# Two rules of buffer and order in the backward pass of a decode block: which free slot a tile takes, and how far dV runs ahead of dK

## The chip, the cores and the metric

The kernel runs on one core of a Trainium2 chip. The metric is the device time of one execution in microseconds (us), the median of several executions; the profile is one more execution, seen by the hardware profiler. The engines are named as in the profile: PE is TensorE, DVE is VectorE, ACT is ScalarE, POOL is GpSimd, and SP is SyncE, which here only issues transfers (its queue is written SPq).

## The reference

The reference runs one decode step of a pre-norm transformer block and takes its gradients. Four sequences (`B = 4`) have one new token each, and each of 32 heads has a cache of 4096 keys and values of width 128:

```python
q = (layernorm(x) @ wq)                       # one query a head and sequence
p = softmax(q . k_cache * Dh**-0.5)           # 4096 weights a head
h = x + (p @ v_cache) @ wo
out = h + (silu(ln(h) @ w1) * (ln(h) @ w3)) @ w2
_out, _vjp = jax.vjp(_f, A_x, A_k_cache, A_v_cache, A_wq, A_wo, B_w1, B_w3, B_w2)
```

It returns `out` and the gradients of all eight inputs. Two of these are as large as the caches: dV (`out_3`) and dK (`out_2`), 4 x 32 x 4096 x 128 in bf16, 1.05 MB (1024 KB) for each of the 128 pairs of sequence and head, which the kernel calls heads. For one head both are outer products: dV is the column p times the row dO (the gradient of the attention output), and dK is the column dS times the row q. dS needs V: dP = V dO, and dS = p (dP - c) scale with a number c for each head. So dV of a head can be made without loading anything, while dK of a head needs V of that head first.

## The kernel before

The forward half (until about 660 us) streams K and V once. A short middle part does the feed-forward block and its backward. The second half, from about 690 us on, loads V once more and writes dV and dK. All large transfers are issued by SP, in the order of the program, on one queue.

**Slots.** All large tiles lie in one SBUF array, `arena`, cut into 23 slots of 8320 bytes a partition (`NSLOT`, `SLOT`). A slot holds one head of K, V, dV or dK. `free` is a list of free slots in the order in which they were given back. `Slot` takes one slot, `Slot2` two neighbouring ones. `give` puts slots at the end of the list as soon as their last use has been written into the program, not when it is over; whoever takes the slot next gets a wait for the work that still holds it. For a slot that held dV or dK this is the landing of the write to HBM.

`Slot` takes the head of the list. While `part["B"]` is set it first calls `lone_slot`, which moves another slot to the head of the list: it prefers the ends of runs of free slots that have an odd length, so that neighbouring slots stay together as pairs for `Slot2`. `Slot2` takes, of the free pairs that its rule allows, the one whose later slot has been free for longest.

**The steps.** Heads 0 to 23 (`SP = 24`) are handled one by one, heads 24 to 127 in 52 pairs (`NT`), which halve the number of transfers and of DVE instructions. `load_V2` loads V of one head, `load_pair` that of two. `front` (or `front_pair`) transposes V on PE, 8 blocks at a time, copies each group of 8 back with ACT (L803 and L804, L1274 and L1275), and multiplies by dO for dP (L1208, L1289). `group_dS` and `group_dS_pair` make dS of four heads on DVE from a transpose of dP that a later `front` puts on PE (`rows_T`). `grad_V` and `grad_K` take a slot, make the outer product with one DVE instruction (`outer`, L809) and issue the write (L820, L1232). `grad_pair` does this for two heads (`outer_pair`, L1355; the write is L1365).

The order of the second half is written out by hand. First five fronts run, with dV of heads 2 to 8 between them. Then step `s` (heads 0 to 23) does: load V, `front(s + 5)`, `more_V(...)`, `grad_K(s)`, and dS at each fourth head. From step 19 on, every second step does the front of a pair. Then step `t` (the 52 pairs) does: loads, `front_pair(t + 3)`, `more_V(...)`, `grad_pair` for dK, and dS at each second pair. `more_V(upto)` writes dV until it is `upto` heads far, and its argument is the number of dK heads done so far plus `lead_V(s)`. `side` adds the small remaining work (the gradient of the weights and of x) between the steps; its outputs go through two-slot tiles (`staged`, L1071).

**What sets the order.** Nothing is rearranged after this: each engine runs its instructions in program order. DVE therefore stops at an outer product whose slot is still being written out, and all later DVE work stops with it. SP stops at a load whose slot is still in use, or at a write whose outer product is not done.

Of the kernel before, what the change touches and what calls it, by code (L numbers as in the profile page):

```python
# [21 lines left out]
SP = 24  # L22
# [3 lines left out]
def kernel(  # L26
# [25 lines left out]
    B = A_x.shape[0]  # L52
# [55 lines left out]
    part = {"B": False}  # L108
# [723 lines left out]
    def load_V2(eng=nc.sync):  # L832
        s = nv["next"]
        if s < SP:
            V2s[s] = Slot("V2", vring if vring else free)
            eng.dma_start(out=V2s[s].heads(), in_=cache_head(A_v_cache, s))
            nv["next"] += 1
# [128 lines left out]
    with ExitStack() as c2:  # L966
# [185 lines left out]
        def replicate(nm_, i0):  # L1152
            if i0 >= NH or (nm_, i0 // REP) in reps:
                return
            K_ = 8 * B if i0 < 8 * B else P
            rows = dOrows_bf if nm_ == "rdo" else qrows_bf
            ps = psrep.tile([P, REP, Dh], FP32, tag="rep", name="rep_ps")
            for i in range(REP):
                nc.tensor.matmul(ps[:, i, :], lhsT=ident_b[0:K_, i0 + i:i0 + i + 1].to_broadcast([K_, P]), rhs=rows[0:K_, :],
                                 start=True, stop=True)  # L1160
            rt = rep_bufs[nm_][i0 // REP % 2]
            nc.scalar.copy(out=rt, in_=ps[:])
            reps[nm_, i0 // REP] = rt
# [28 lines left out]
        def front(s):  # L1192
            hl = s % B
            if s not in VTs:
                for g in range(SJ // GW):
                    V_T(s, psT, range(g, g + 1))
                    if hl == 0 and g == 0:
                        rows_out()
                    if hl == 0 and g == 2:
                        rows_T()  # L1200
            VT = VTs[s].heads()
            if hl == 0:
                rows["acc"] = psD.tile([P, 512], FP32, tag="dP", name="dP_ps")
            dO_window(s + 2)
            for u in range(2):
                for c in range(4):
                    j0 = 8 * c + 4 * u
                    nc.tensor.matmul(rows["acc"][32 * c:32 * (c + 1), :], lhsT=zq_window(zd[hl], 2 * hl + u),  # L1208
                                     rhs=VT[:, j0:j0 + 4, :], start=(hl == 0 and u == 0),
                                     stop=(hl == B - 1 and u == 1), tile_position=(0, 32 * c))  # L1210
            if hl == B - 1:
                rows["ps"] = rows.pop("acc")
            sl = VTs.pop(s)
            (vring if nv["next"] < SP and len(V2s) + len(VTs) + len(vring) < NV2 else free).append(sl.i)

        def group_dS(g):
            i0 = g * B
            T = rows.pop("T").rearrange("p jj (c m) -> p c m jj", c=4)
            t = rows.pop("t")[:, 0:B * SJ].rearrange("p (b j) -> p b j", b=B)
            t5 = t.rearrange("p b (c u jj) -> p b c u jj", c=4, u=2)  # L1220
            for hl in range(B):
                nc.vector.tensor_scalar(out=t5[:, hl], in0=T[:, :, 2 * hl:2 * hl + 2, :], scalar1=c_rep[:, i0 + hl:i0 + hl + 1],
                                        scalar2=scale, op0=ALU.subtract, op1=ALU.mult)
            dS2s[g] = bw3.tile([P, B, SJ, 2], BF16, tag="dS2", name="dS2", bufs=1)
            nc.vector.tensor_tensor(out=dS2s[g][:], in0=t[:, :, :, None].to_broadcast([P, B, SJ, 2]),
                                    in1=P_all[:, i0:i0 + B, :, None].to_broadcast([P, B, SJ, 2]), op=ALU.mult)

        def grad_K(s):
            b, h = bh_of(s)
            gk = Slot("gk")  # L1230
            outer(gk.heads(), dS2s[s // B][:, s % B], reps["rq", s // REP][:, s % REP, :])
            nc.sync.dma_start(out=rows_of(out_2[b, h]), in_=gk.heads())  # L1232
            gk.give()

        def prefetch():
            while nv["next"] < SP and vring:
                load_V2(nc.sync)
# [21 lines left out]
        def load_pairs(t):  # L1259
            while npv["next"] < NT and (npv["next"] <= t or len(pV) < 3 and len(Slot2.choices()) > 1):  # L1260
                load_pair()

        def dO_pair(t):
            if t < NT:
                s, s2 = two(t)
                nc.gpsimd.tensor_copy(out=zt[t % B][:, 32:34], in_=dOT_bf[:, s:s2 + 1:B])

        def front_pair(t, mid):
            pl = t % 2
            v = pV[t].t[:, 0:2 * SJ * Dh].rearrange("p (j d) -> p j d", d=Dh)  # L1270
            for g in range(2 * SJ // GW):
                pt = psT.tile([P, GW, P], BF16, tag="tps", name="pt_tps")
                for i in range(GW):
                    nc.tensor.transpose(pt[:, i, :], v[:, g * GW + i, :], ident_b[:])  # L1274
                nc.scalar.copy(out=v[:, g * GW:(g + 1) * GW, :], in_=pt[:])  # L1275
                if pl == 0 and g == 0:
                    rows_out()
                if pl == 0 and g == 2:
                    rows_T()
                if g == 3:  # L1280
                    mid()
            if pl == 0:
                rows["acc"] = psD.tile([P, 512], FP32, tag="dP", name="dP_ps")
            dO_pair(t + 2)
            for u in range(4):
                m = 8 * pl + 2 * u
                for c in range(4):
                    j0 = 16 * c + 4 * u
                    nc.tensor.matmul(rows["acc"][32 * c:32 * (c + 1), :], lhsT=zt[t % B][:, 32 - m:64 - m], rhs=v[:, j0:j0 + 4, :],  # L1289
                                     start=(pl == 0 and u == 0), stop=(pl == 1 and u == 3), tile_position=(0, 32 * c))  # L1290
            if pl == 1:
                rows["ps"] = rows.pop("acc")
            pV.pop(t).give()
# [38 lines left out]
        def replicate_pair(nm_, q):  # L1332
            if q >= NT // B or (nm_, "p", q) in reps:
                return
            s = SP + q * 2 * B
            K_ = 8 * B if s + 2 * B <= 8 * B else P
            rws = dOrows_bf if nm_ == "rdo" else qrows_bf
            ps = psrep.tile([P, REP, Dh], FP32, tag="rep", name="rep_ps")
            for i in range(REP):
                for a in range(2):  # L1340
                    n = s + i + a * B
                    nc.tensor.matmul(ps[64 * a:64 * (a + 1), i, :], lhsT=ident_b[0:K_, n:n + 1].to_broadcast([K_, P // 2]),
                                     rhs=rws[0:K_, :], start=True, stop=True, tile_position=(0, 64 * a))
            rt = rep_bufs[nm_][(H0 + q) % 2]
            nc.scalar.copy(out=rt, in_=ps[:])
            reps[nm_, "p", q] = rt
# [45 lines left out]
                    replicate_pair("rdo", t // B + 1)  # L1392

        def lead_V(s):
            return 8 - min(4, max(0, s - 56) // 4)

        def load_ahead(s):
            prefetch()
            if s < SP and s not in V2s and s not in VTs:
                load_V2(nc.sync)  # L1400

        def side(s):
            if O0 <= s < S0:
                step("o")
            if s >= S1:
                step("s", 2)
            elif s >= O0:
                step("q")

        part["B"] = True  # L1410
        for s in range(2):
            dO_window(s)
        for s in range(3, 6):
# [9 lines left out]
                replicate("rdo", REP)  # L1423
        group_dS(0)
        for s in range(SP):
            load_ahead(s + L)
            if nv["next"] >= SP:
                load_pairs((s + L - SP) // 2)
            if s % REP == 2:
                if s + 2 < SP:  # L1430
                    replicate("rq", s + 2)
                else:
                    replicate_pair("rq", 0)
            if s + L < SP:
                front(s + L)
            elif (s + L - SP) % 2 == 0:
                if s + L == SP:
                    dO_pair(0)
                    dO_pair(1)
                front_pair((s + L - SP) // 2, lambda: None)  # L1440
            if s > 0:
                more_V(s + 1 + lead_V(s))
            grad_K(s)
            if s % B == B - 1:
                if s + 1 < SP:
                    group_dS((s + 1) // B)
                else:
                    group_dS_pair(0)
            side(s)
        for t in range(NT):  # L1450
            s = SP + 2 * t
# [46 lines left out]
```

## Time and profile before

Three executions gave a median of 1730.34 us (1726.66 to 1730.5); the profiled one has a span of 1731.4 us.

| what | number |
|---|---|
| HBM read and written | 422.59 MB and 282.34 MB, 407 GB/s over the span |
| busy share of the 16 DMA engines, SP's queue | 98.1% |
| PE busy | 1240.6 us (72%) |
| DVE busy | 1231.9 us (71%) |
| ACT busy | 959.4 us (55%) |
| DVE outer product, one head (L809) | 2.29 us |
| DVE outer product, one pair (L1355) | 4.42 us |
| share of the chain that ended last: DMA out_dram<-arena | 38% |

The busy share of DMA is a mean of 16 engines; the GB/s beside it tell whether the engines moved data at the pace that they show elsewhere. A stretch in which the pace is lower is one in which time is lost for good, if the transfers are what the kernel must wait for. The chain that ended last is followed back from the last instruction; a step "DMA out_dram<-arena" in it means that an instruction waited for a write to HBM to land.

### The profile page before, as it was taken

The page shows a single profiled execution, that of the slowest core. Times are in us where ns is not written, and L with a number is a line of the kernel's source. Part 1 is how long each engine was busy: PE and PEld are TensorE (multiplying, and loading weights), DVE is VectorE, ACT ScalarE, POOL GpSimd, SP SyncE. Part 2 cuts the span into 40 slices and gives each one's busy share as a digit, 9 for nine tenths or more (in the row PEclk, how much of TensorE's full clock was granted, in tenths as well). Part 3 has the DMA queues.
Part 4 walks back from the last instruction along what each step waited for, and adds up shares of the span by engine and source line. Part 5 has one row for each costly group of instructions (what it writes and reads, how often), then busy time and mean ns, then how long its engine had stood idle before and what let it go on. Part 6 is the DMA issues. An engine that isn't in the chain of part 4 may idle for free.

```text
span 1731.4 us, 37799 instructions
## 1 busy us (share of the span) xinstructions
PE 1240.6 (72%) x16232; PEld 954.3 (55%) x16232; DVE 1231.9 (71%) x1190; ACT 959.4 (55%) x1489; POOL 318.3 (18%) x575
## 2 busy tenths in 40 slices
PE   5889888888888889766788655666656756766550
PEld 4677766677667667544566544544434434444340
DVE  5999899989999995456586666565546475475584
ACT  3555455445455445565667466666657656655540
POOL 2211222322222221102103021012003011011030
PEclk9999999999999998897878689867788666666865
DMA  9999999999999999699989999999999999999997
GB/s 401 424 425 424 424 423 425 423 423 424 417 420 407 424 413 401 251 385 385 427 362 425 430 427 428 428 426 430 426 396 406 427 419 401 414 407 401 402 406 337
DMA packets 78264, 707.45 MB, mean 409 GB/s; under 512 B 8444, under 2 KB 12680, under 8 KB 14224
## 3 DMA queue, kind: packets, MB, share of 16 engines
q1 hardware_dynamic: 77680, 704.94, 98.1%
q8 instruction: 127, 2.08, 0.5%
q14 instruction: 41, 0.34, 0.0%
q0 software_dynamic: 416, 0.10, 0.0%
HBM read 422.59 MB, written 282.34 MB: 407 GB/s over the span
## 4 chain that ended last, share of the span: by engine, by line
DMA 41%; DVE 13%; issue 3%; PE 3%; ACT 1%; DVEq 0%; SPq 0%; POOL 0%; ACTq 0%
DMA out_dram<-arena 38%; DVE arena L1355 8%; DMA arena<-in_A_v_cache_dram 4%; DVE arena L809 3%; ACT arena L1275 1%; PE M_ps L475 1%; DVE arena L460 1%; PE pt_w L604 1%; PE pt_tps L1274 0%; ACT Pn L439 0%; DVEq L1493 0%; PE kP_ps L485 0%; DVE dPr L1302 0%; PE gu_ps L876 0%; PE dn_ps L907 0%
## 5 line engine op out<-in xcount | busy, mean ns | idle before, releaser
L1275 ACT COPY arena<-pt_tps 128x1024 bf16<-128x1024 bf16 x416 | 400.2, 1023 | 234.1 <-PE pt_tps L1274 233.5
L1274 PE MATMUL pt_tps<-ident_b,arena 128*128 128x128 bf16 x3328 | 328.2, 269 | 223.8 <-DMA arena<-in_A_v_cache_dram 147.7
L1274 PEld LDWEIGHTS <-arena 128*128 128x128 bf16 x3328 | 282.1, 124 | 321.4 <-DMA arena<-in_A_v_cache_dram 168.9
L1355 DVE TENSOR_TENSOR arena<-arena 128x8192 bf16<-128x8192 bf16 x52 | 230.0, 4423 | 183.9 <-DMA out_dram<-arena 168.3
L1355 DVE TENSOR_TENSOR arena<-dS,arena 128x8192 bf16<-128x8192 bf16 x52 | 230.0, 4425 | 120.9 <-DMA out_dram<-arena 120.7
L475 PE MATMUL M_ps<-arena 128*128 128x130 bf16 x4096 | 286.4, 222 | 35.4 <-DMA arena<-in_A_v_cache_dram 35.2
L460 DVE TENSOR_TENSOR arena<-arena 128x4096 bf16<-128x4096 bf16 x128 | 292.5, 2285 | 24.7 <-POOL arena L456 23.6
L475 PEld LDWEIGHTS <-arena 128*128 128x128 bf16 x4096 | 253.4, 99 | 55.7 <-DMA arena<-in_A_v_cache_dram 48.6
L367 DVE STREAM_TRANSPOSE arena<-arena 128x512 f32<-128x512 f32 (+1 forms) x321 | 250.7, 797 | 0.0
L362 ACT COPY arena<-pt_tps 128x1024 bf16<-128x1024 bf16 x128 | 129.4, 1012 | 183.5 <-PE pt_tps L361 145.1
L1352 POOL COPY arena<-arena 128x128 bf16<-128x128 bf16 x52 | 78.1, 1502 | 562.3 <-ACT arena L1329 300.9
L373 POOL TENSOR_TENSOR W<-qrep,wmask 128x128 bf16<-128x128 bf16 x128 | 121.0, 945 | 85.3 <-PE S_ps L393 70.7
L456 POOL COPY arena<-P_all 128x64 bf16<-128x64 bf16 x128 | 32.7, 255 | 412.5 <-ACT P_all L450 409.5
L804 ACT COPY arena<-pt_tps 128x1024 bf16<-128x1024 bf16 x96 | 91.9, 1024 | 19.5 <-PE pt_tps L803 19.3
L1289 PE MATMUL dP_ps<-arena 128*32 128x512 bf16 x832 | 91.4, 473 | 9.2 <-ACT arena L1275 9.1
L803 PE MATMUL pt_tps<-ident_b,arena 128*128 128x128 bf16 x768 | 64.9, 244 | 32.9 <-ACT arena L804 27.9
L450 ACT COPY P_all<-pt_P 32x64 bf16<-32x64 bf16 x256 | 52.1, 203 | 54.1 <-PE pt_P L446 51.9
L361 PE MATMUL pt_tps<-ident_b,arena 128*128 128x128 bf16 x1024 | 80.5, 223 | 0.0
L485 PE MATMUL kP_ps<-arena,onesw 128*32 128x512 bf16 x1024 | 79.2, 386 | 0.0
L803 PEld LDWEIGHTS <-arena 128*128 128x128 bf16 x768 | 56.0, 112 | 41.3 <-issue 40.0
L809 DVE TENSOR_TENSOR arena<-P,arena 128x4096 bf16<-128x4096 bf16 x21 | 48.0, 2290 | 43.2 <-DMA out_dram<-arena 43.0
L809 DVE TENSOR_TENSOR arena<-dS,arena 128x4096 bf16<-128x4096 bf16 x24 | 54.9, 2295 | 31.6 <-DMA out_dram<-arena 31.5
(245 smaller groups left out, 1534.5 us busy)
## 6 DMA issues: line engine op xcount, KB each, us to landing
out_dram<-arena SPq DMA_DIRECT2D x108, 2048.0 KB, 21.5
arena<-in_A_v_cache_dram SPq DMA_DIRECT2D x152, 1024.0 KB, 15.5
arena<-in_A_k_cache_dram SPq DMA_DIRECT2D x128, 1024.0 KB, 15.4
arena<-in_A_v_cache_dram SPq DMA_DIRECT2D x52, 2048.0 KB, 24.4
out_dram<-arena SPq DMA_DIRECT2D x48, 1024.0 KB, 8.1
arena<-in_A_wq_dram SPq DMA_DIRECT2D x8, 1024.0 KB, 17.3
arena<-in_B_w_dram SPq DMA_DIRECT2D x8, 896.0 KB, 15.5
out_dram<-arena SPq DMA_DIRECT2D x3, 1792.0 KB, 25.2
```

The costliest lines, as they stand in the source:

```text
L362: nc.scalar.copy(out=KT[:, c * GW:(c + 1) * GW, :], in_=pt[:])
L367: nc.vector.transpose(out=KT[:, c * w_:(c + n) * w_], in_=Kn[:, c * w_:(c + n) * w_])
L373: nc.gpsimd.tensor_tensor(out=W[:, hl], in0=qrep[:, :, s:s + 1].to_broadcast([P, 4, 32]), in1=wmask[:, hl, None, :].to_broadcast([P, 4, 32 ...
L460: nc.vector.tensor_tensor(out=PK[:, :, 0:Dh].rearrange("p j (r t) -> p j r t", t=2), in0=Ks[s].heads().rearrange("p j (r t) -> p j r t", t=2),
L475: nc.tensor.matmul(hold["M"][:], lhsT=Vn[:, j, :], rhs=PK[:, j, :], start=(j == 0), stop=(j == SJ - 1))
L803: nc.tensor.transpose(pt[:, i, :], v[:, g * GW + i, :], ident_b[:])
L804: nc.scalar.copy(out=v[:, g * GW:(g + 1) * GW, :], in_=pt[:])
L809: nc.vector.tensor_tensor(out=dst.rearrange("p j (r t) -> p j r t", t=2), in0=col2[:, :, None, :].to_broadcast([P, SJ, Dh // 2, 2]), in1=r ...
L1274: nc.tensor.transpose(pt[:, i, :], v[:, g * GW + i, :], ident_b[:])
L1275: nc.scalar.copy(out=v[:, g * GW:(g + 1) * GW, :], in_=pt[:])
L1289: nc.tensor.matmul(rows["acc"][32 * c:32 * (c + 1), :], lhsT=zt[t % B][:, 32 - m:64 - m], rhs=v[:, j0:j0 + 4, :], start=(pl == 0 and u == ...
L1355: nc.vector.tensor_tensor(out=dst.rearrange("p (j r t) -> p j r t", r=Dh // 2, t=2), in0=col2[:, :, None, :].to_broadcast([P, 2 * SJ, Dh / ...
```

## The change

The change has two parts.

1. `part["B"]` was set to true ahead of the first step of the second half and stayed so. Now it is set in each step `s` of the single heads, to `s + 12 >= SP`. So in the five fronts before the steps, and in the steps 0 to 11, `Slot` takes the slot that was given back first; from step 12 on (twelve heads ahead of the change to pairs) and through all pairs, `lone_slot` chooses as before. It is for a longer time between the write of a slot and the next use of that slot.
2. `lead_V(s)` was 8 heads up to head 56 and went down to 4 from head 72 on. Now it is 8 to the end. dV of the later heads is made two pairs earlier, and the last steps have dK alone.

```diff
         def lead_V(s):
-            return 8 - min(4, max(0, s - 56) // 4)
+            return 8
...
-        part["B"] = True
         for s in range(2):
             dO_window(s)
...
         group_dS(0)
         for s in range(SP):
+            part["B"] = s + 12 >= SP
             load_ahead(s + L)
```

No transfer, no outer product and no matmul is added or removed. What differs is which slot a tile lies in, what its first instruction has to wait for, and in what order dV, dK and loads follow each other from head 60 on.

## The prediction

> **What bounds the kernel now.** I first read the DMA row of the page, then cut the span into stretches, then looked at the chain of waits where a stretch is slow. The stretches (length; busy us and count of PE, PE weight load, DVE, ACT and POOL; granted clock; DMA share; GB/s):
>
> ```profile
> 700.00:740.00 40.00, 27.18 (x268) 17.49 (x266) 19.70 (x17) 26.28 (x30) 7.47 (x24) 0.83 0.62 236
> 740.00:840.00 100.00, 67.56 (x751) 49.71 (x746) 63.69 (x47) 58.89 (x67) 18.56 (x25) 0.85 0.99 394
> 840.00:920.00 80.00, 61.39 (x654) 47.90 (x655) 50.31 (x37) 51.31 (x60) 6.92 (x18) 0.81 0.95 394
> 920.00:1240.00 320.00, 208.84 (x2188) 156.52 (x2186) 197.13 (x105) 201.55 (x238) 62.53 (x47) 0.79 1.01 428
> 1240.00:1320.00 80.00, 49.00 (x544) 33.16 (x542) 49.50 (x28) 53.62 (x67) 13.35 (x13) 0.84 0.97 398
> 1400.00:1660.00 260.00, 164.10 (x1421) 113.49 (x1419) 147.03 (x67) 156.11 (x199) 22.67 (x29) 0.69 1.00 407
> ```
>
> For 320 us the transfers run at 428 GB/s with every engine under 70%: the second half is bound by transfers. I use 428 GB/s as the pace that can be had. Time lost in a stretch is its length times (1 - GB/s / 428): 18 us in 700 to 740, 8 in 740 to 840, 6 in 840 to 920, 6 in 1240 to 1320, 13 in 1400 to 1660. The first is by far the densest, and the chain of waits there (start, length, what) is
>
> ```profile
> 702.63 7.46 DMA out_dram<-arena
> 710.22 2.30 DVE arena L809
> 712.53 3.85 DMA out_dram<-arena
> 716.51 2.30 DVE arena L809
> 718.83 3.85 DMA out_dram<-arena
> 722.80 2.30 DVE arena L809
> 725.12 3.93 DMA out_dram<-arena
> 729.17 2.30 DVE arena L809
> ```
>
> An outer product, its write to HBM, then the next outer product: strictly in turn. DVE waits for the write that still holds its slot. I followed the free list through both programs (bookkeeping, in which no time enters) and numbered SP's transfers from 0; dV of head 0 is number 279. Before, numbers 281, 282 and 283 (dV of heads 2, 3, 4) all take slot 0, each right behind the last. Up to number 310 dV and dK then alternate mostly between slots 0 and 2, used again 2 to 4 transfers later, mostly 3. The waits in 700 to 740 say the same (engine, line, for what: us, times, longest):
>
> ```profile
> DVE arena L809 <- DMA out_dram<-arena: 19.8, 6, 7.5
> ACT arena L1162 <- DVE arena L809: 3.7, 1, 3.7
> ```
>
> The first line is the wait for slots; the second is a knock-on, a row replica that ACT can't overwrite before the late DVE has read it, and PE's transposes wait behind it.
>
> **What the Trainium skill says.** (1) "Perfetto Trace Analysis", section "Optimization Strategy": the same gap again and again on the engine that should be full can mean that there was no buffer for the next tile. The trace agrees: three waits of 3.85 to 3.93 us in a row. (2) "DMA: Bandwidth & Descriptors", section "Anatomy of one DMA": about 2.0 us fixed, mostly the receipt of the last byte, beside bytes over 436 GB/s; waits are taken by the issuing sequencer, never by the DMA engines. Here a lone write of 1.05 MB lands after 3.85 us, which at 428 GB/s is 2.45 us of data and 1.40 us fixed; I use the trace. (3) The same page, section "Queues, rings and completion order": descriptors are consumed in ring order. So the depth of SP's queue counts: a wait for a landing is hidden while other transfers stand in the queue. The 3.85 us waits stand where it was empty; later pair loads took 24.4 us (median) to land, a full queue.
>
> **Part 1, first slots in order of being freed: 700 to 740.** Now numbers 281 to 285 rotate over slots 10, 11 and 0, used again 3 transfers later. One turn of a slot is 2.30 us of DVE and 3.85 us to the landing; three slots give one head each (2.30 + 3.85) / 3 = 2.05 us, under the 2.45 us that its data takes. So the transfers become the bound here too. Until 709 the queue is full in any case with loads of V. From there numbers 281 to 290, seven dV and three V, need 10 x 2.45 = 24.5 us, to 733. The next, dK of head 0 (number 291), needs dS of the first group, thus the transposes in front 4. Undisturbed fronts start 5.0 us apart (730.35 and 735.35 before); front 1 starts at 704.96 as before, so front 4 at 720 to 721, its `rows_T` at 724, dS 0.72 + 0.42 us later, dK issued at 728, 5 us ahead of the drain. Before it was issued at 745.18. I count 3 of the 18 us as still lost: **-15 us**.
>
> **Part 1, 740 to 840.** Numbers 287 to 324 are now used again after 6 to 9 transfers (before: 3 for most, 4 to 6 from 311 on). Each step moves one dV, one dK and one V: 3 x 2.45 = 7.35 us. DVE needs 2 x 2.30 us and a quarter of 1.14, 4.9 us. PE and ACT need 6.3 us for a front with its side work (fronts started at 754.10, 760.40 and 767.09 when nothing held them up), so they keep ahead by about 1 us a step, with three bundles of dO columns of some 3 us each to take out of it over 19 heads. Neither is the bound, though with little room. The stretch 920 to 1240, where slots come back after 6 or 7 transfers, loses nothing. I take 5 of the 8 us: **-5 us**.
>
> **Part 1, 840 to 920.** From number 333 to 412 both programs have the same transfers in the same slots, with uses again after 3 to 5 transfers at the change to pairs. This stretch should come some 20 us earlier and lose its 6 us again: 0.
>
> **Part 2, the lead.** Two dV pairs move from the end to the steps of heads 60 and 68. Before, the second of these steps has one write only (issued at 1270.29), and the next dV takes the slots of a weight gradient written 3 transfers earlier:
>
> ```profile
> 1289.37 4.42 DVE L1355 TENSOR_TENSOR arena<-arena 128x8192 bf16<-128x8192 bf16 x1 [19.11 <-DMA out_dram<-arena]
> 1274.08 0.90 ACT L1096 COPY arena<-pt_Tr 4x896 bf16<-4x896 bf16 x1 [14.64 <-DMA out_dram<-arena]
> ```
>
> DVE waits 19.11 us and the queue runs dry from 1290 to 1296 (153 to 286 GB/s, some 3 us lost). Now the step has two writes, and it is a load (number 428) that takes these slots. That adds a wait to SP: the load waits for the landing of number 425, and the writes 429 and 430 stand behind it, with DVE's later slots. When 425 lands, 426 and 427 (2 x 4.9 us of data) are still queued, so the DMA engines should not run dry. ACT's wait of 14.64 us stays: in both programs the slot of `rows1` was given back 2 transfers earlier, and fronts queue behind it. I take **-2 us**, between -3 (the whole gap) and +5 (SP's wait shows).
>
> Elsewhere in the pairs slots come back after 4 or 5 transfers in both programs, so I leave the 13 us of 1400 to 1660 as they are. **The tail**: before, ten writes follow the last load, now eight. The last load was issued at 1660.14, its transposes began at 1681.28 and its `rows_T` ended at 1692.1, 32 us after the issue. Now six outer products and one dS stand between load and last dS, 28.8 us after the issue; DVE waits 3 us, and the last dK is issued 42.5 us after the load. The queue, which before drained at 1722, 62 us after the load, drains two writes sooner, at 52 us. So 9 us of room stay; 0.
>
> **Sum**: 1730.3 - 15 - 5 - 2 = 1708 us.
>
> **The rivals.** *A, given back later.* The early gain only makes the transfers arrive at a slower place: PE and ACT with 1 us a step of room, or the short reuse at 333 to 342, where the queue drains deeper. Then half of the 15 us and nothing of the 5 stay: 1730.3 - 8 = 1722. For it: 20 us are gained on engines whose room is small; against it: 320 us at 428 GB/s behind it. *B, the late pace too.* 1400 to 1660 has a DMA share of 1.00 and yet 407 GB/s, with the lead at 4; 920 to 1240 had 428 with the lead at 8. If the lead is the cause, most of the 13 us come on top: 1708 - 11 = 1697. Against it: 1320 to 1400 ran at 427 GB/s with the lead at 4 already. *C, not faster.* The first half of A, and SP's load wait or the thin tail costs as much as the rest brings: 1730. *D, slower.* PE's fronts set the pace from 740 on, so that nothing early remains, and SP's wait and an unhidden tail cost 5 us each: 1740.
>
> **How the numbers follow.** Forecast 0.60, A 0.14, B 0.12, C 0.06, D 0.08. The predicted time is the forecast's, 1708. The range takes in A and B with some room for the +5 of part 2 and for a run's spread: 1694 to 1725. Faster is forecast, A and B: 0.86; within 0.3%: 0.06; slower: 0.08.
>
> **What would show it.** In 700 to 740 the pace should be near 400 GB/s, the slot waits of L809 down from 19.8 us to some 8, and the first dK (L1232) issued near 728. 740 to 820 should run above 410 GB/s. The load that waits on SP should show beside a DMA share of 1.0. If PE is the bound in 740 to 840, PE's idle time vanishes there and the pace stays below 400: then A. The prediction is wrong if 700 to 740 is fast and the span is not some 15 us shorter, or if the end of the chain becomes dS.

## The result, and the profile after

| kernel | median us (lowest to highest) | ratio to before [95% interval] |
|---|---|---|
| before | 1730.42 (1726.66 to 1730.88) | |
| changed | 1704.17 (1697.57 to 1709.01, 4 runs) | 0.985 [0.981, 0.990] |
| changed, measured again | 1707.07 (1699.05 to 1709.31, 4 runs) | 0.986 [0.984, 0.988] |

The forecast was 1708 us. One thing to keep in mind below: the eight times of the changed kernel lie in two groups, three from 1697.6 to 1699.6 and five from 1706.2 to 1709.3, and both profiles taken of it (spans 1707.2 and 1707.5 us) belong to the second.

The stretches of the changed kernel, with the columns of the table in the prediction (length; busy us and count of PE, PE weight load, DVE, ACT, POOL; granted clock; DMA share; GB/s):

```profile
700.00:740.00 40.00, 29.23 (x310) 19.15 (x308) 29.25 (x22) 29.36 (x34) 16.05 (x27) 0.88 0.97 389
740.00:840.00 100.00, 78.21 (x863) 58.64 (x861) 61.29 (x47) 68.86 (x80) 23.94 (x31) 0.90 1.01 426
840.00:920.00 80.00, 62.83 (x718) 48.64 (x718) 60.90 (x38) 55.61 (x65) 17.36 (x13) 0.87 0.96 395
920.00:1240.00 320.00, 208.85 (x2092) 155.30 (x2091) 192.61 (x103) 197.44 (x236) 39.42 (x42) 0.75 1.01 428
1240.00:1320.00 80.00, 50.09 (x510) 34.00 (x508) 49.33 (x27) 50.15 (x64) 15.57 (x14) 0.76 1.01 421
1320.00:1400.00 80.00, 55.06 (x452) 37.28 (x450) 46.92 (x20) 49.94 (x66) 8.87 (x16) 0.65 1.00 412
1400.00:1660.00 260.00, 161.41 (x1412) 114.69 (x1410) 152.59 (x73) 154.31 (x195) 24.11 (x27) 0.69 1.00 405
```

The first row went from 236 to 389 GB/s, the second from 394 to 426. The third and the last stayed. (The rows are cut by time: behind 840 us the changed kernel is some 22 us ahead, so that the same row holds later transfers than before.) Where DVE was in strict turn with its writes, its timeline (start, length, what, and in brackets the idle time before it and its releaser) now reads:

```profile
707.36 2.29 DVE L809 TENSOR_TENSOR arena<-P,arena 128x4096 bf16<-128x4096 bf16 x1 [0.35 <-DMA out_dram<-arena]
709.83 2.29 DVE L809 TENSOR_TENSOR arena<-P,arena 128x4096 bf16<-128x4096 bf16 x1 [0.18 <-DMA out_dram<-arena]
712.34 2.29 DVE L809 TENSOR_TENSOR arena<-P,arena 128x4096 bf16<-128x4096 bf16 x1 [0.22 <-DMA out_dram<-arena]
714.80 6.73 DVE L809 TENSOR_TENSOR arena<-P,arena 128x4096 bf16<-128x4096 bf16 x3 [0.16 <-DMA out_dram<-arena]
```

Gaps of 0.16 to 0.35 us stand where waits of 3.85 us stood: one outer product every 2.47 us, which is the pace of the transfers. The waits for slots in this window (us in total, times, longest), and SP's issue of the first dK:

```profile
DVE arena L809 <- DMA out_dram<-arena: 6.1, 6, 2.6
```

```profile
727.61 0.33 SPq L1232 DMA_DIRECT2D out_dram<-arena  x1
```

Before, the waits were 19.8 us and that dK left at 745.18. So at transfer 291 the changed kernel is 17.6 us ahead. Comparing the issue of the same transfer in the two traces, the lead is 23.0 us at number 300, 25.7 at 328, 22.1 at 340 and 22.3 at 412, and the span ends 24.2 us earlier. Comparing the landings, it is 22.1 us at 328, 22.1 at 340, 22.2 at 412, 24.3 at 430 and 24.1 at the last. The gain is made before 840 us, and all of it lasts; the last 2 us come between 412 and 430.

### The profile page after: what moved, and what is told of

Its sections match the earlier page's. It is cut to its first block, busy times and chain, and to the rows that moved or that the text cites. A ratio compares the mean times of both kernels' runs of the same rounds, so it can differ in the third digit from the quotient of the medians.

```text
span 1707.2 us, 37798 instructions
## 1 busy us (share of the span) xinstructions
PE 1247.2 (73%) x16232; PEld 959.9 (56%) x16232; DVE 1232.0 (72%) x1190; ACT 958.9 (56%) x1489; POOL 314.0 (18%) x575
## 5 line engine op out<-in xcount | busy, mean ns | idle before, releaser
L1274 PE MATMUL pt_tps<-ident_b,arena 128*128 128x128 bf16 x3328 | 333.9, 272 | 220.8 <-DMA arena<-in_A_v_cache_dram 148.8
L1274 PEld LDWEIGHTS <-arena 128*128 128x128 bf16 x3328 | 288.0, 126 | 323.7 <-DMA arena<-in_A_v_cache_dram 174.6
L475 PEld LDWEIGHTS <-arena 128*128 128x128 bf16 x4096 | 253.8, 99 | 58.4 <-DMA arena<-in_A_v_cache_dram 50.5
L1352 POOL COPY arena<-arena 128x128 bf16<-128x128 bf16 x52 | 71.5, 1376 | 598.2 <-DVE arena L1355 380.8
L803 PE MATMUL pt_tps<-ident_b,arena 128*128 128x128 bf16 x768 | 64.2, 242 | 24.6 <-ACT arena L804 20.4
L361 PE MATMUL pt_tps<-ident_b,arena 128*128 128x128 bf16 x1024 | 80.5, 223 | 0.0
L361 PEld LDWEIGHTS <-arena 128*128 128x128 bf16 x1024 | 62.0, 100 | 25.9 <-issue 25.8
L393 PE MATMUL S_ps<-arena,W 128*32 128x256 bf16 x1536 | 75.2, 285 | 0.5 <-DVE arena L367 0.2
## 6 DMA issues: line engine op xcount, KB each, us to landing
out_dram<-arena SPq DMA_DIRECT2D x108, 2048.0 KB, 21.2
```

The lines of the kernel that those rows point to most:

```text
L361: nc.tensor.transpose(pt[:, i, :], Kn[:, c * GW + i, :], ident_b[:])
L475: nc.tensor.matmul(hold["M"][:], lhsT=Vn[:, j, :], rhs=PK[:, j, :], start=(j == 0), stop=(j == SJ - 1))
```

## The experiments

**The two parts, and the fronts alone.** The first kernel has the new order of slots with the old lead, the second the old order with a lead of eight; the third ends the order by age right after the five fronts. The changed kernel was measured again beside them (its row is above). All diffs here are against the changed kernel.

```diff
 e1:  def lead_V(s):
-         return 8
+         return 8 - min(4, max(0, s - 56) // 4)
 e2:  part["B"] = True        # before the fronts, for good, as in the kernel before
 e3:  group_dS(0)
+     part["B"] = True
      for s in range(SP):
-         part["B"] = s + 12 >= SP
```

> Part 1 alone: slots in order of being freed until step 11, the lead still falling from 8 to 4. Theory (the gain is the removed wait for slots ahead of 840 us): transfer number 410 is issued some 22 us earlier than before, as in the changed kernel, and the span is about 1708 us; the dip of three us near the second weight gradient stays. Rival (the lead makes a good part of the gain): about 1715 us.

> Part 2 alone: lead 8 to the end, slots chosen as before. Theory: 2 us faster than before (1728 us), nothing before number 413 moves. Rival (the lead also cures the late pace, or costs by SP's wait for a load): 1718 us, or 1735 us.

> The first half of part 1 with part 2: slots in order of being freed during the five fronts ahead of the steps alone, from step 0 on as before. Theory: the 15 us of 700 to 740 are won, the 5 to 8 us of 740 to 840 stay lost: about 1711 us. Rival A (transfers only arrive earlier at a slower place and the first gain is given back there): over 1716 us. If all of the gain came from the first five fronts: 1706 us.

> The changed kernel once more, on the same chip as the others, for its spread: four executions lay at 1698, 1700, 1709 and 1709 us. If this is two ways of running, both groups show again and a profile of the faster one differs in the late stretch, 1240 to 1660; if it is chance, the values fill the gap.

| kernel | median us (lowest to highest) | ratio to before [95% interval] | ahead at transfer 412, us |
|---|---|---|---|
| slots alone | 1710.38 (1708.67 to 1711.71) | 0.988 [0.987, 0.990] | 21 |
| lead alone | 1728.47 (1718.85 to 1733.42, 22 runs) | 0.999 [0.998, 1.000] | 1 |
| slots in the fronts alone, lead of eight | 1712.95 (1709.57 to 1713.4) | 0.989 [0.988, 0.991] | 17 |

Part 1 is the gain; part 2 alone is at the edge of what can be told from no change. The third kernel came near the 1711 us expected of it. The repeat showed both groups of times again, but its profile too was of the slower one: no run of 1698 to 1700 us of the changed kernel was profiled. With the order by age in the fronts only, 740 to 840 falls back to the pace of before:

```profile
740.00:840.00 100.00, 73.37 (x810) 54.38 (x810) 61.09 (x47) 64.13 (x75) 25.37 (x32) 0.87 0.98 393
```

So 17 us come from the fronts and 5 from the steps 0 to 11. In that same window the changed kernel's DVE waited 40.2 us for slots, more than this one's 36.3. What tells them apart is the queue: 426 GB/s at a DMA share of 1.01 against 393 at 0.98.

**The late pace.** From 1400 us on the changed kernel moves 405 GB/s, as before, although the DMA share is 1.00. Four kernels bear on it. One has the order by age until four heads ahead of the change to pairs, and was made for the stretch 840 to 920; one has a lead that grows to twelve, and was made for the end. The other two were to find out why the late pace is low: one in which two free pairs of slots are held idle from pair step 2 to 14, so that slots are used again sooner there; one that loads V two pairs ahead, not three.

```diff
 e4:  part["B"] = s + 4 >= SP
 e5:  return 8 + min(4, max(0, s - 56) // 4)
 e6:  if t == 2: idle = [Slot2() for _ in range(2)]
      if t == 14: [sl.give() for sl in idle]
 e7:  while ... (npv["next"] <= t or len(pV) < 2 and len(Slot2.choices()) > 1):
```

> The changed kernel with slots in order of being freed until step 19 instead of 11. Writes 333 to 342 then come back after 4 to 10 transfers instead of 3 to 5, but the first pair load takes a slot written 2 transfers earlier. Theory (the 6 us of 840 to 920 are lost to short reuse): 3 us faster than the changed kernel, and L1232 writes closer together. Rival (SP's wait for that load stops the writes behind it): 2 to 5 us slower than it.

> The changed kernel with a lead that rises from 8 to 12 heads after head 56, so that six writes instead of eight follow the last load. Theory of the tail: the queue would drain 42 us after the last load, but the last dS can't be made earlier (32 us to the end of its transposes), so that the last two writes are issued at 38 and 43 us: 6 us slower than the changed kernel. Rival (the tail has more room than I think): no slower. In the changed kernel DVE already waits 3.3 us for the last dS.

> The changed kernel with two pairs of slots held idle from pair step 2 to 14, so that writes there come back after 4 transfers instead of 6 or 7, as they do late in both kernels. Theory (the late pace of 405 GB/s is due to the short reuse): the stretch 960 to 1160 falls from 428 to some 405 GB/s, 10 us slower. Rival (the late pace has to do with the addresses, the weight gradients or the mix there): 428 GB/s stays, no slower.

> The changed kernel with at most two V pairs loaded ahead by the early rule instead of three, which frees slots: late writes come back after 5 to 7 transfers instead of 4 or 5. If short reuse sets the late pace: 1400 to 1640 rises from 405 towards 420 GB/s, up to 8 us faster. Rival: the pace stays, or the fronts wait longer for their loads and it is slower.

The medians were 1701.94, 1698.99, 1701.33 and 1701.61 us (ratios 0.984 [0.982, 0.986], 0.982 [0.980, 0.984], 0.984 [0.982, 0.985], 0.984 [0.982, 0.986]). To their own questions: the first had gained nothing by transfer 412 (20.5 us ahead, the changed kernel 22.3 and 21.2), so its theory fell. The third was to bring the slow pace to 960 to 1160 by reuse after 4 transfers, and did so by nearly half: 419 GB/s, where 405 was expected and the changed kernel has 429. The fourth did as the reuse theory said, and the second, which was to lengthen the end, was in total 5 to 8 us faster than the changed kernel.

All four ran 424 to 427 GB/s in 1400 to 1640. Of the first two nobody had expected it, and in the third it came long after the slots were given back: four such different edits must share something that the theories had not named. The row of the lead of twelve and the changed kernel's, for the same stretch:

```profile
1400.00:1640.00 240.00, 158.38 (x1373) 109.26 (x1373) 142.23 (x65) 151.11 (x192) 39.63 (x27) 0.69 1.01 427
```

```profile
1400.00:1640.00 240.00, 153.29 (x1328) 108.54 (x1326) 132.70 (x63) 146.54 (x186) 19.69 (x26) 0.68 1.00 408
```

Both read as a full DMA. The Trainium skill says in "Perfetto Trace Analysis", section "Identifying the Most-Contended Engine", that the occupancy of 16 DMA engines misleads and that the bytes moved should be used; these two lines are a case of it.

**A wrong suspect.** What the others had in common (before, changed, and the first three experiments) was ACT's wait of 14.3 to 14.7 us at L1096, for the slot of `rows1`; the four did not have it. Three kernels put that to the test: the changed one with an old slot for `rows1`; the one with a lead of twelve with a slot for `rows1` written 2 transfers earlier; and three edits together.

```diff
 e8:
+     part["B"] = False
      r1, r2 = Slot("rows1"), Slot("rows2")
+     part["B"] = True
 e9, on e5:
+     free.remove(4); free.appendleft(4); part["B"] = False
      r1, r2 = Slot("rows1"), Slot("rows2")
+     part["B"] = True
 e10: e5 and e8 together, and part["B"] = s + 4 >= SP
```

> The changed kernel, with the slot of rows1 taken by age: slot 5, last written by transfer 416, instead of slot 10, last written by transfer 422. Nothing else is meant to move; later slots shift by a place. Theory S (ACT's wait of 14.6 us at L1096 brings the late slow pace): the wait is gone (below 3 us), the pace in 1400 to 1640 goes from 405 to about 425 GB/s, and the time to about 1700 us (1698 to 1703), with no run near 1707. Theory R (the wait and the slow pace only occur together; the pace is decided by where dK writes and V loads meet, or by chance): the wait is gone, but the pace stays at 405 to 410 GB/s and the time at 1706 to 1708 us.

> The kernel with a lead of twelve (1699 us, no wait of ACT at L1096, 427 GB/s late), but rows1 is given a slot that was written 2 transfers earlier (slot 4, transfer 424). Theory S: ACT waits 10 to 15 us at its copy into rows1, the pace in 1400 to 1640 falls to about 405 GB/s, and the time goes to about 1707 us (+8). Theory R: ACT waits as long, but the pace stays at 425 GB/s, and the time at 1699 to 1701 us.

> Three edits together: lead of twelve at the end, slots by age until four heads ahead of the change to pairs, and the slot of rows1 by age. Theory S: no wait at L1096, late pace 425 GB/s or more; the lead of twelve and the later change of order each gain nothing beyond the late pace: about 1698 us (1694 to 1701). Theory R: the late pace is either value, 1698 or 1706 us.

The medians were 1703.6, 1703.4 and 1709.55 us (0.984 [0.983, 0.986], 0.984 [0.983, 0.985], 0.987 [0.985, 0.989]). The first had lost the wait and ran at 418 GB/s, between the two theories. The second had the wait, and longer:

```profile
ACT arena L1100 <- DMA out_dram<-arena: 24.0, 1, 24.0
```

```profile
1400.00:1640.00 240.00, 150.90 (x1365) 105.13 (x1364) 137.12 (x65) 149.18 (x190) 17.96 (x27) 0.73 1.01 423
```

and still ran at 423 GB/s. The third had no such wait, and yet the old pace; as a whole it came out slower than the lead of twelve by itself:

```profile
1400.00:1640.00 240.00, 152.70 (x1331) 106.07 (x1328) 137.99 (x64) 147.65 (x189) 17.97 (x27) 0.71 1.00 405
```

The theory of the wait falls. The two had only gone together.

**When the transfers were issued.** SP's queue ends each transfer with one packet of 4 bytes on each of the 16 engines: the trace of the changed kernel has 8176 of them, 511 transfers times 16. ("DMA: Bandwidth & Descriptors", section "Why a DMA increments its semaphore by 16 and not by 1", says that each of the engines ends its share with its own write to the semaphore; the count agrees.)

These packets do not name their transfer. Put in order of time and cut into sixteens, they tell how much of the queue's work is done: a transfer is 16 shares, one for each engine, and at the first packet of the sixteen of transfer n, 15 shares are left of everything up to n. The measure used here is how long before that moment transfer n + 1 has been issued; the time of a transfer is that from the end of one sixteen to the end of the next. Worked out for the transfers 440 to 499 of the 14 profiles at hand (before, changed and all experiments; the few that took under 4.6 us, weight gradients among them, are left out), with a mark of 2.25 us that was set before the last experiment ran, and with the other 13 at hand, this gives:

```
issued before only 15 shares were left           transfers   mean us   median us
under 2.25 us (or after it)                            168      5.39        5.31
over 2.25 us, but the next one under                   127      5.22        5.10
over 2.25 us, and so the next one                      503      4.88        4.86
```

Late issues go with slow transfers. By kernel, for the same 60 transfers (late: under 2.25 us; lost: the time over 4.86 us each; the fifth column is explained below):

| kernel | writes to a slot written 4 or fewer transfers earlier | late | lost, us | last engine behind the other 15, us | GB/s, 1400 to 1640 |
|---|---|---|---|---|---|
| before | 14 | 17 | 17.9 | 6.1 | 406 |
| changed (two profiles) | 13 | 16, 17 | 18.0, 17.0 | 6.8, 6.5 | 408, 410 |
| slots alone | 14 | 14 | 18.5 | 6.3 | 405 |
| lead alone (its run of 1718.85 us) | 13 | 17 | 7.5 | 3.8 | 419 |
| slots in the fronts alone | 13 | 15 | 16.0 | 6.0 | 409 |
| slots to head 20 | 0 | 10 | 4.4 | 7.4 | 424 |
| lead of twelve | 0 | 7 | 3.4 | 6.3 | 427 |
| two pairs held | 0 | 9 | 3.9 | 7.0 | 425 |
| two loads ahead | 0 | 2 | 5.4 | 1.2 | 425 |
| old slot for rows1 | 8 | 11 | 9.8 | 5.6 | 418 |
| new slot for rows1, lead of twelve | 15 | 9 | 6.5 | 2.8 | 423 |
| three edits | 14 | 16 | 17.9 | 7.0 | 405 |

The four kernels do have one thing in common: no write of this stretch takes a slot that was written 4 transfers earlier; 5 is the least. They have 2 to 10 late issues and lose 3.4 to 5.4 us. With reuse after 4, DVE waits for the slot and the write follows late: 9 to 17 late issues, 6.5 to 18.5 us. (The 6.5 are those of the kernel with the new slot for rows1: 15 such writes, but only 9 late issues. It is the lateness that goes with the loss; reuse after 4 makes it likely.) The prediction had counted "4 or 5 transfers in both programs" and passed over it.

The fifth column sorts the same ends by transfer. SP's transfers count on eight semaphores in turn, so each semaphore gives 16 ends to every eighth transfer. In the changed kernel the first 15 ends of a transfer lie within 2.6 us (mean of 440 to 499), and the last comes 6.8 us after them: one engine is behind. The lag grows in the second half, from 0.5 us in the transfers 355 to 364 over 3.8 in 405 to 414 to 7.8 in 495 to 504. At the end of the span the other 15 are done, and a DMA share of 0.06, one engine of sixteen, is left for 6.7 us:

```profile
1700.00:1706.00 6.00, 0.00 (x0) 0.00 (x0) 0.00 (x0) 0.00 (x0) 0.00 (x0) 0.50 0.06 25
```

DVE waits until all 16 ends are there. Transfer 464 of the changed kernel had 15 of its ends by 1463.79 us and the last at 1470.17; the outer product that takes its slot 4 transfers later starts right behind, so that its wait is all lag:

```profile
1470.26 4.42 DVE L1355 TENSOR_TENSOR arena<-dS,arena 128x8192 bf16<-128x8192 bf16 x1 [6.46 <-DMA out_dram<-arena]
```

The column also sorts the exceptions: among the kernels with 13 to 15 such writes, those with a lag of 6.0 us or more lose 16 us or more, those with 2.8 and 3.8 lose 6.5 and 7.5. And in the kernel with two pairs held, where 13 writes of the transfers 345 to 410 take slots again after 3 or 4, the lag there was 1.3 us, and the pace fell to 419 GB/s and not to 405. In the lead of twelve the other 15 engines ran dry at the end as expected (done at 1676.7 us, the next write issued at 1684.06), but meanwhile the last one caught up and ended only 1.4 us after them. No kernel was made to test the lag, and why one engine falls behind is open.

Why 4 in one and 5 in the other? By the free list of the changed kernel all free slots lie in pairs when `rows2` is taken, 5-6 among them; it takes 5, the end that had been free for longest, and holds it through the stretch. Slot 4, when it comes back, finds no neighbour, and a pair is missing from the rotation. The last experiment changes that one number: `rows2` in slot 6, so that 4 and 5 make a pair again, and `rows1` left in slot 10.

```diff
-     r1, r2 = Slot("rows1"), Slot("rows2")
+     r1 = Slot("rows1")
+     free.remove(6); free.appendleft(6); part["B"] = False
+     r2 = Slot("rows2")
+     part["B"] = True
```

> The changed kernel with one slot number other: rows2 lies in slot 6 instead of slot 5; rows1 stays in slot 10. Slot 5 was half of the pair 4-5, so a ninth pair of slots now goes round in the late stretch: of the transfers 440 to 499, 13 writes take slots written 4 transfers earlier in the changed kernel, none here (13 at 5, 9 at 6, the rest last loaded). Theory P (reuse after 4 transfers issues a write too late, so that the first of the 16 DMA engines to finish have to wait for it, inside packets that count as busy): late pace 420 to 428 GB/s in 1400 to 1640, transfers 440 to 499 lose 3 to 7 us over 4.86 us each instead of 18, issues that come under 2.25 us before the first engine is done with the transfer in front 5 to 10 of 60 instead of 16; time 1698 to 1702 us, with no run near 1707; ACT still waits 14 to 15 us at L1096. Theory S (that wait of ACT is the cause): the wait stays and so does 405 to 410 GB/s, 1706 to 1708 us. Theory R (chance): some runs near 1699, some near 1707, as the changed kernel has.

It took 1698.84 us (1698.31 to 1699.13, 5 runs), ratio 0.9815 [0.980, 0.983]; of the 60 transfers 8 were late and 3.3 us lost. ACT's wait is still there:

```profile
ACT arena L1101 <- DMA out_dram<-arena: 14.7, 1, 14.7
```

```profile
1400.00:1640.00 240.00, 150.29 (x1321) 103.58 (x1319) 144.72 (x71) 145.08 (x184) 41.61 (x30) 0.71 1.01 426
```

SP's issues of a few steps (start, length of a group, what), first in the changed kernel, then in this one; L1365 and L1370 are the same write:

```profile
1449.86 9.96 SPq L1365 DMA_DIRECT2D out_dram<-arena  x2
1460.08 0.34 SPq L1257 DMA_DIRECT2D arena<-in_A_v_cache_dram  x1
1463.83 11.22 SPq L1365 DMA_DIRECT2D out_dram<-arena  x2
1475.58 0.34 SPq L1257 DMA_DIRECT2D arena<-in_A_v_cache_dram  x1
```

```profile
1445.92 4.67 SPq L1370 DMA_DIRECT2D out_dram<-arena  x2
1451.38 0.34 SPq L1262 DMA_DIRECT2D arena<-in_A_v_cache_dram  x1
1460.92 4.76 SPq L1370 DMA_DIRECT2D out_dram<-arena  x2
1466.33 0.34 SPq L1262 DMA_DIRECT2D arena<-in_A_v_cache_dram  x1
```

In the changed kernel dV and dK are issued 9.6 and 10.9 us apart, because DVE waits for a slot between them; in this one 4.3 and 4.4 us, one DVE instruction after the other. DVE's slot waits from 1400 to 1640, changed kernel and this one (total, times, longest):

```profile
DVE arena L1355 <- DMA out_dram<-arena: 109.7, 15, 12.2
```

```profile
DVE arena L1360 <- DMA out_dram<-arena: 88.8, 17, 6.3
```

In total DVE waits nearly as long, but no wait exceeds 6.3 us. Theory P has held in time, pace, lost time and late issues, and the two rivals have fallen: all five times lie under 1699.2 us with ACT's wait in place, and none near 1707, where five of the changed kernel's eight had been. What it did not show is its clause on how the time is lost. It spoke of the first engines to finish, by sixteens that mix the lagging engine's ends with those of the next transfer. In the changed kernel only part of the loss is engines without work: around 1440 us the packets in flight fall from 16 to 6, and over 1400 to 1640 some 2.4 us of all engines' time are without a packet. Most is in packets of 16 KB that take longer than the usual 0.611 us, up to 2.26, with work queued. Losses over 6 us come only with 9 or more late issues, in these profiles, but the run of the lead alone has 17 and lost 7.5 us: late issue does not set the size alone. Why the packets stretch stays open; so does what makes one run of the changed kernel take 1699 us and the next 1708.

## Why the prediction was right

- **Fronts, -15 us.** Held. Pace 389 GB/s (near 400 predicted), 40 x (1 - 389 / 428) = 3.6 us lost (3 predicted), slot waits 6.1 us (8), first dK at 727.61 (728). The fronts alone are worth 17 us at transfer 412. (The 2.0 us quoted from "Anatomy of one DMA" stand there for transfers that GpSimd issues; here SP issues them, and the prediction went by its own 1.40 us.)
- **740 to 840, -5 us.** Held, and put a little low: the pace was 426 GB/s, so 0.5 us were lost and not 3. Neither PE nor ACT became the bound (78.2 and 68.9 us busy of 100). The steps 0 to 11 are worth 22 - 17 = 5 us by transfer 412.
- **840 to 920, 0.** Held by its pace (395 GB/s against 394). The lead in issues fell from 25.7 us at transfer 328 to 22.1 at 340, where slots are used again after 3 to 5 transfers; the lead in landings was 22.1 us at both. So nothing was given back, and rival A fell.
- **The lead of dV, -2 us.** Held. DVE's waits for slots from 1240 to 1320 went from 34.1 us (the longest 19.11) to 19.2 (the longest is the first line). Loads waited on SP, but no longer than before (8.5 us in total there), and the queue stayed full, with a DMA share of 1.00 or 1.01 in every 10 us:

```profile
1261.61 4.42 DVE L1355 TENSOR_TENSOR arena<-dS,arena 128x8192 bf16<-128x8192 bf16 x1 [8.82 <-DMA out_dram<-arena]
```

```profile
SPq L1257 <- DMA out_dram<-arena: 7.3, 3, 5.0
```

  The lead in landings rose from 22.2 us at transfer 412 to 24.3 at 430 and stayed; in the kernel with the slots alone it was 21.3 at both. ACT's wait at L1096 stayed at 14.7 us, as predicted, but fronts queueing behind it cost nothing that the runs show.
- **The tail, 0.** Held. DVE waited 3.30 us for the last dS (3 predicted), and the last write left 42.8 us after the last load (42.5), 9.0 us before the first engine was through with the whole queue (9):

```profile
1678.07 1.18 DVE L1302 TENSOR_SCALAR dPr<-dPT_ps,c_rep 64x64 f32<-64x64 f32 x4 [3.30 <-PE dPT_ps L1190]
```

  One sign that the prediction had set against itself did come: the chain followed back from the last instruction now goes from DVE's last outer product through this dS to PE and ACT. It cost nothing, because the first engine to finish still had work for 4.1 us when the last write was issued. What the prediction took for the end of the queue (52 us after the last load) is the end of 15 engines (51.8 to 53.8); the sixteenth needed 60.5. It was as late before (7.4 us behind the others, 6.7 now), so the difference was right.

- **The sum.** Part 1 was put at 20 us, thus 1710 us without part 2; it measured 1710.38. With both, 1708 was predicted, and 1704.17 and 1707.07 were measured. Part of this nearness is luck: by transfer 412 part 1 had brought 22 us and not 20, and three of eight runs took 1698 to 1700 us, 8 to 10 us less than the forecast, which no term of it accounts for.
- **Rival B** took the shorter lead for the cause of the late pace. With a lead of eight the pace is 408 GB/s, so it fell, though its time, 1697, can be had by other means, and three of the changed kernel's own runs came within 3 us of it. The prediction left the 13 us of 1400 to 1660 as they are, which is what the change did, but its reason hid the cause: reuse after 4 and after 5 transfers are not the same thing there. Rivals C and D fell too: PE was no bound, and neither SP's waits nor the end cost anything that the runs show.

## What to carry to other kernels

Count, in transfers, how long a buffer rests between its write and its next use: a rest of 3 transfers where the same slot had been taken right behind the last write gave 17 us here, and in the late stretch one slot number that made 4 into 5 took the pace from 408 to 426 GB/s, though reuse after 4 went with 419 and 423 in two profiles, those in which the last engine lagged less. A full DMA share is no proof of a full queue; look at GB/s and at how early transfers are issued. And where neighbouring slots are needed, a small long-lived tile in half of a pair takes the whole pair away: its place is worth choosing (one slot number: 1698.84 us, where five of eight runs had taken 1706 to 1709).

## What had not been expected of the hardware

- Packets stretch, and the share of busy time does not show it. "Perfetto Trace Analysis", section "DMA Engine Tracks", has it that slices show busy time without idle; that leaves out that they can be slow: here packets of the same 16 KB on the same queue take 0.611 us as a rule, but in 1400 to 1640 of the changed kernel 192 of 5737 took over 1 us, up to 2.26 (in 960 to 1160, 10 of 5075), and the DMA share reads 1.00 at 405 GB/s and 1.01 at 426.
- One of the 16 engines of a queue can fall behind by more than a whole transfer of 2.1 MB: on the mean of the transfers 495 to 504 by 7.8 us in the changed kernel and by 10.1 in the last experiment. In both it works alone at the end, for 6.7 and 10.5 us at 25 GB/s, and the mean busy share does not show it before that.
